# Two transformer layers on one core: a new order for the first transfers and norms, and order tables by segment

## The chip, the cores and the metric

The kernel runs on one core of a Trainium2 chip. The time is the device time of one execution in microseconds (us); lower is better. The engines of a core are TensorE (PE in the profile), VectorE (DVE), ScalarE (ACT), GpSimd (POOL) and SyncE (SP). SP and ACT issue the transfers (DMAs) from the chip's main memory. PE multiplies; only DVE and ACT bring results out of its accumulators, the PSUM banks.

## What is computed

One attention block and one gated feed-forward block, twice in a row with the same weights, over a sequence of 2048 rows of width 512:

```
x = x + attention(layernorm(x)) @ wo      # 32 heads of width 16; a row sees itself and the 255 rows before it
x = x + (sigmoid(g) * u) @ w_down         # g = layernorm(x) @ w_gate, u = layernorm(x) @ w_up, width 1792
```

The layernorm has no scale and no offset and adds 1e-5 to the variance. Queries, keys and values are three slices of `layernorm(x) @ wqkv`; scores are scaled by 1/4.

## The kernel before

**Tiles.** The 2048 rows are 16 tiles of 128; four tiles are a group. x stays in on-chip memory (`xsb`), and so do all weights. A tile's path is: statistics of x on DVE (`BATCH_NORM_STATS2`, L589, then the aggregate, L590; for the first four tiles also the addition of 1e-5, L592), the power -1/2 on POOL (L598, L599), the normalised tile on DVE (L617), its transpose (four PE matmuls at L638 and a copy, L666 on ACT or L668 on DVE; later tiles go by a transposing DMA), then the products for queries (L703), keys (L734) and values (L770). A key tile is copied out and split into even and odd heads by two DVE products (L749).

**Score visits.** Attention runs in 77 visits per layer, 154 in all, each a block of small score matmuls (L1029, L1040, L1050) into four PSUM banks (`Sps`), one exponential of 128x2048 on ACT (L1082, 1.88 us) and mask products on DVE (L960). The values products (L1109) follow when a half tile's exponentials and masks are done. Then come the normalisation by the row sums, the output product (L893), the addition into x (L899), the second norm, the gate and up products (L798), tanh on ACT (L816) and the product on DVE (L824), and the down product (L862) with its addition into x (L871) and, in the second layer, the store (L878).

**The order is planned by the program that writes the kernel.** `Plan` simulates the engines while the instructions are emitted: each task has a set of engines, a duration written by hand, dependencies and a priority; when an engine is free in the plan, the ready task with the lowest priority number is emitted there next. On the chip each engine executes in the emitted order, and waits where something it needs is late. So every constant of the plan (durations, `LAND` and `SLACK` for the landing of transfers, `COLD`, `SWITCH`, `PACE`) acts on the time only through the order. `Net.pick` fills PE: when a visit is due (`pace` after the last one, or as soon as the last exponential is done and there is nothing else) its scores are emitted; otherwise a unit of dense products is chosen by `rank`. With nothing to do it emits `keep_warm` matmuls (L1292) whose results are not used. The tables before are two, one for visits 0 to 23 and one for the rest (`PRIO`, `SLACK`, `RANK`; `LATE_...`); `PACE` has a spacing of 1600 ns for visits 0 to 11, 2511 to visit 23, then 2682 in the first layer and 3207 in the second.

**The first transfers** (`loads`, all issued at L455): x tile 0, x tile 1, x tiles 2 and 3, then the key weights and the query weights; each is halved, one half on SP's queue and one on ACT's. The value weights (512 KB) are whole on ACT's queue. Then SP's queue alone brings x tiles 4 to 7, `wo`, x tiles 8 to 11, the gate and up weights, and, after a planned delay, x tiles 12 to 15 and the down weights in seven parts. The first key and query units work tile by tile (three key chunks, two query chunks); the others need all four tiles.

**Gate and up by groups of tiles** (`glu_units`, `GLU`): `GLU[1][OPT["g2"]]` is [4, 4, 4, 2, 2] in the second layer, so its last four tiles are two groups of two with matmuls of 256 columns.

Of the kernel before, what the change touches and what calls it, by code (L numbers as in the profile page):

```python
# [12 lines left out]
P = 128  # L13
# [43 lines left out]
def pool_ns(n):  # L57
# [5 lines left out]
GLU = [[[1] * 4 + [4], [1] * 4 + [2] * 2, [1] * 6 + [2], [1] * 8, [2] * 4, [1] * 2 + [2] * 3, [2] * 2 + [4]], [[4] * 3 + [2, 1, 1], [4] * 3 + [2, 2], [4] * 4]]  # L63
PACE = [2682, 3207, 1600, 2511, 23.52]
# [6 lines left out]
COLD = 5200  # L71
SWITCH = 96
LAND = 1230
RATE = ((3300, 330.0), (5300, 160.0), (1e9, 345.0))
# [7 lines left out]
PRIO = dict(st_x0=7.13, ap_x0=2.72, xt_x0=3.36, st_x1=-0.44, ap_x1=1.86, xt_x1=6.58, st_x=18.87, ap_x=6.56,  # L82
    xt_x=2.0, st_p=7.13, ap_p=4.46, xt_p=0.81, st_g=2.23, ap_g=1.32, xt_g=6.14, st_g0=5.97, ap_g0=3.21,
    xt_g0=1.33, tp=5.75, tp_g=-0.06, q=4.0, q0=5.51, q1=4.74, k=1.95, k0=-0.89, k1=-1.49, s=-1.15, s0=5.46,
    s1=3.28, v=0.28, v0=5.43, v1=14.72, vv=5.53, exp=3.64, exp0=4.71, m0=4.61, m00=-0.56, e0=1.11, e00=1.28,
    e1=7.21, e10=6.56, m2=0.64, m20=3.6, th=5.12, mu=-0.12, dn=1.29, add=-0.27, add0=1.8, out=-2.4, mv=5.8,
    mv0=6.23, oq=-2.27, oq0=-0.14, no=4.71, no0=2.61, on=5.93, on0=0.59, vc=9.2, vc0=-0.87)
OPT = dict(gu='SP', g1=1, bk=3, bq=2, wide=0, r0=2, g0=1, g2=1, x0=1, eps=1, hold=0, own=1, ck=0, cq=2,
    turn=2)
SLACK = dict(xt=1208, oq=843, on=211, vc=1208)  # L90
RANK = dict(tp=-1.708, o=-2, lead=14.747, far=7.411, v=9.3, g=1.778, d=1.823, feed=11.672, x3=21097, wd=474,
    go=364)
LATE_PRIO = dict(st_p=-0.04, ap_p=7.96, xt_p=-0.99, st_x=1.07, ap_x=4.81, xt_x=-1.16, st_g=1.75, ap_g=1.19,
    xt_g=2.76, q=3.84, k=4.33, s=4.05, v=0.61, exp=1.12, m0=4.62, e0=2.79, e1=4.39, m2=5.49, th=1.65, mu=2.51,
    dn=2.1, add=0.69, out=0.45, mv=3.49, oq=0.77, no=6.44, on=2.16, vc=0.22)
LATE_SLACK = dict(xt=489, oq=1327, on=2346, vc=897)
LATE_RANK = dict(tp=-2, o=1.576, lead=9.722, far=6.159, v=1.796, g=1.769, d=3.896, feed=7.551, go=1418)

class Late(dict):


    def __missing__(self, name):
        return {"vv": self["v"], "tp": 0, "tp_g": 2}[name] if name in ("vv", "tp", "tp_g") else self[name[:-1]]

# [262 lines left out]
class Net:  # L369
# [74 lines left out]
    def loads(self, A_x, wqkv, wo, w_gate, w_up, w_down):  # L444
# [31 lines left out]
        for t, n in {1: ((0, 1), (1, 1), (2, 2)), 2: ((0, 2), (2, 2)), 3: ((0, 1), (1, 3))}[OPT["x0"]]:  # L476
            ev = load_x(self.xsb[:, t:t + n, :], slice(t, t + n), n, 0, ("SP", "ACT"))
            for i in range(t, t + n):
                self.has_x[i] = ev
        if OPT["wide"]:  # L480
            self.has_wq["q"] = self.has_wq["k"] = both([
                load(self.wq[:, k:k + 2, 0:2 * D], wq_src[:, k:k + 2, 0:2 * D], 4 * P * D * 2, prio=0, queue=q, row=4 * D)
                for k, q in ((0, "ACT"), (2, "SP"))])
        else:
            for w in "kq":
                h = slice("qk".index(w) * D, ("qk".index(w) + 1) * D)
                self.has_wq[w] = both([load(self.wq[:, k:k + 2, h], wq_src[:, k:k + 2, h], 2 * P * D * 2, prio=0, queue=q)
                                       for k, q in ((0, "ACT"), (2, "SP"))])
        self.has_wq["v"] = load(self.wq[:, :, 2 * D:3 * D], wq_src[:, :, 2 * D:3 * D], D * D * 2, prio=0, queue="ACT")
# [14 lines left out]
    def constants(self):  # L504
        nc = self.nc
        nc.gpsimd.memset(self.nhalf[:], -0.5)
# [10 lines left out]
        for i in range(2):  # L517
            self.zeros(0, i)
        self.pl.free["POOL"] = 3000.0
        self.pl.free["SP"] = self.pl.free["ACT"] = 750.0  # L520
        self.pl.at(750.0)
        self.pl.at(1500.0)
        self.pl.free["DVE"] = 3600.0
        self.pl.at(3600.0)
# [11 lines left out]
    def later_constants(self):  # L536
# [23 lines left out]
        for i in range(2):  # L560
            self.vzero[i] = pl.task({"POOL": 800}, lambda e, i=i: self.zeros(1, i), first, prio=8, port=True).done
# [7 lines left out]
    def layer_norm(self, key, t, deps):  # L569
# [15 lines left out]
        def stats(e):  # L585
            if "st" not in box:
                box["st"] = self.take("st")
            st = box["st"][0][:, mine]
            nc.vector.bn_stats(out=st[:, 0:6], in_=self.xsb[:, t, :])  # L589
            nc.vector.bn_aggr(out=st[:, 6:8], in_=st[:, 0:6])  # L590
            if first:
                nc.vector.tensor_scalar(out=st[:, 9:10], in0=st[:, 7:8], scalar1=1e-5, scalar2=None, op0=ALU.add)  # L592
# [29 lines left out]
        a = pl.task({"DVE": 910 + 70 * first}, stats, deps, self.prio["st_" + kind], lambda: "st" in box or self.has("st"))  # L622
# [11 lines left out]
        if alone:  # L634
# [6 lines left out]
            def evac(u):  # L641
                pt = self.tp_view(u.bank)
# [29 lines left out]
    @property  # L672
    def prio(self):
        return PRIO if self.slot < PACE[4] else Late(LATE_PRIO)

    @property
    def slack(self):
        return SLACK if self.slot < PACE[4] else LATE_SLACK

    @property  # L680
    def ranks(self):
        return RANK if self.slot < PACE[4] else LATE_RANK
# [839 lines left out]
```

The softmax here doesn't subtract the row's maximum and nothing guards it: scores larger than these inputs give would overflow.

## Time and profile before

| | us |
|---|---|
| median of 3 runs | 541.87 (541.84 to 542.01) |
| span of the profiled execution, first to last instruction | 539.6 |
| PE busy in the span | 531.1 (98%) |
| DVE busy | 420.5 (78%) |
| ACT busy | 382.3 (71%) |
| POOL busy | 43.4 (8%) |
| first score visit, first matmul at | 13.49 |
| last score visit | 470.77 |

The profiled execution is one execution; its span leaves out about 2.3 us that lie around it in the timed runs. "Busy" for PE takes in the modelled drain of each matmul, so a short gap between two matmuls' starts can be hidden in it; the spacing of starts in the timeline is sharper. A group's "idle before" is the time in which its engine had nothing running just before such an instruction, with what ended it. In the timeline a row is a run of like instructions: start, length, engine, line, operation, operands and how many.

### The profile page before, as it was taken

To read this page: it belongs to the slowest core of one execution; us is meant where nothing else is said; L and a number is where in the kernel's file an instruction comes from. 1 tells how busy PE (TensorE), PEld (TensorE's weight loads), DVE (VectorE), ACT (ScalarE), POOL (GpSimd) and SP (SyncE) were. 2 spreads that over 40 slices of the span, in tenths; PEclk is the share of its full clock that TensorE was granted. 3 is DMA by queue.
4 is the path that set the end of the run, shared out by engine and by line. 5 is a ranking of instruction groups with operands and counts; after the bars stand their busy time and mean duration, and the time that the engine had idled before them with its cause. 6 is when DMAs were issued, how large, how long until landed. Compare 5 with 4: busy or idle time off the path is not lost.

```text
span 539.6 us, 21359 instructions
## 1 busy us (share of the span) xinstructions
PE 531.1 (98%) x9658; PEld 293.0 (54%) x9658; DVE 420.5 (78%) x844; ACT 382.3 (71%) x380; POOL 43.4 (8%) x99
## 2 busy tenths in 40 slices
PE   8999999999999999999999999999999999999997
PEld 8446755855767444544444444544444444455873
DVE  6999999789878997798977789778677785674442
ACT  4989989878888687776778767787667866540330
POOL 5301110001000110101100010101000000000000
PEclk9999999999999999999999999999999999999999
DMA  8890334232421323143110622117211241132001
GB/s 260 317 227 15 43 72 57 50 61 63 72 52 33 72 51 60 36 101 59 32 35 14 105 51 47 38 42 108 54 45 28 60 72 50 24 70 58 2 11 39
DMA packets 95067, 36.23 MB, mean 67 GB/s; under 512 B 78336, under 2 KB 93952, under 8 KB 94976
## 3 DMA queue, kind: packets, MB, share of 16 engines
q1 hardware_dynamic: 93600, 33.56, 29.9%
q8 instruction: 75, 1.23, 1.0%
q10 hardware_dynamic: 1376, 1.31, 0.8%
q14 instruction: 16, 0.13, 0.1%
HBM read 9.70 MB, written 2.10 MB: 22 GB/s over the span
## 4 chain that ended last, share of the span: by engine, by line
PE 89%; DVE 5%; ACT 2%; DMA 1%; issue 1%; POOL 0%; SPq 0%; ACTq 0%; POOLq 0%
PE bank L798 37%; PE bank L862 18%; PE bank L1109 9%; PE Sps L1029 7%; PE bank L893 5%; PE bank L734 4%; PE bank L770 3%; PE bank L703 3%; PE Sps L1040 2%; ACT PTring L1082 1%; DMA wq<-in_A_wqkv_dram 1%; DVE kTp L749 1%; DVE st L589 1%; DVE PTring L960 1%; DVE edge L960 1%
## 5 line engine op out<-in xcount | busy, mean ns | idle before, releaser
L1082 ACT ACTIVATE PTring<-Sps 128x2048 bf16<-128x2048 f32 (+1 forms) x122 | 226.0, 1852 | 63.2 <-PE Sps L1029 59.2
L798 PE MATMUL bank<-xnT,wu 128*128 128x512 bf16 (+2 forms) x728 | 128.2, 297 | 0.0
L798 PE MATMUL bank<-xnT,wg 128*128 128x512 bf16 (+2 forms) x728 | 128.2, 298 | 0.0
L862 PE MATMUL bank<-wd,hT 128*128 128x512 bf16 (+2 forms) x462 | 109.9, 373 | 0.0
L824 DVE SCALAR_TENSOR_TENSOR hT<-hT,bank 128x256 bf16<-128x256 bf16 (+1 forms) x154 | 80.8, 537 | 34.0 <-ACT hT L816 21.2
L816 ACT ACTIVATE hT<-bank 128x256 bf16<-128x256 f32 (+1 forms) x154 | 71.1, 482 | 48.5 <-PE bank L798 47.8
L798 PEld LDWEIGHTS <-wg 128*128 128x128 bf16 x728 | 60.7, 98 | 36.7 <-issue 2.3
L798 PEld LDWEIGHTS <-wu 128*128 128x128 bf16 x728 | 61.4, 98 | 34.5 <-issue 2.5
L1082 ACT ACTIVATE edge<-Sps 128x2048 bf16<-128x2048 f32 (+1 forms) x32 | 56.6, 1770 | 17.3 <-PE Sps L1040 17.3
L862 PEld LDWEIGHTS <-hT 128*128 128x128 bf16 x462 | 43.0, 98 | 46.4 <-issue 2.2
L668 DVE CAST OTs<-bank 128x512 bf16<-128x512 f32 x59 | 43.0, 729 | 21.5 <-PE bank L1109 21.1
L960 DVE TENSOR_TENSOR PTring<-PTring,mask 128x1024 bf16<-128x1024 bf16 x64 | 43.7, 684 | 12.3 <-ACT PTring L1082 12.1
L1109 PE MATMUL bank<-PTring,Vaug 128*32 128x64 bf16 (+1 forms) x2880 | 52.0, 203 | 0.0
L1109 PEld LDWEIGHTS <-Vaug 128*32 128x32 bf16 x2880 | 44.0, 97 | 12.0 <-issue 10.4
L1029 PE MATMUL Sps<-qT,kTp 32*128 32x256 bf16 (+3 forms) x1216 | 47.4, 248 | 1.2 <-ACT PTring L1082 1.1
L598 POOL TENSOR_SCALAR st<-st 128x2 f32<-128x2 f32 (+1 forms) x33 | 10.7, 325 | 443.6 <-DVE st L590 443.6
L589 DVE BATCH_NORM_STATS2 st<-xsb 128x6 f32<-128x512 bf16 x64 | 43.9, 686 | 1.7 <-DMA xsb<-in_A_x_dram 1.2
L1109 PE MATMUL bank<-edge,Vl 128*32 128x64 bf16 x1024 | 44.4, 193 | 0.1
L960 DVE TENSOR_TENSOR edge<-edge,maske 128x1024 bf16<-128x1024 bf16 x60 | 40.3, 682 | 3.4 <-ACT edge L1082 3.3
L1029 PEld LDWEIGHTS <-kTp 32*128 32x128 bf16 x1216 | 18.2, 92 | 45.4 <-issue 43.5
L1109 PE MATMUL bank<-edge,Vh 128*32 128x64 bf16 x896 | 40.8, 193 | 0.0
L960 DVE TENSOR_TENSOR PTring<-PTring,maskn 128x1024 bf16<-128x1024 bf16 x56 | 38.2, 682 | 0.0
(73 smaller groups left out, 522.0 us busy)
## 6 DMA issues: line engine op xcount, KB each, us to landing
Vl<-Vaug SPq DMA_DIRECT2D x32, 68.0 KB, 2.4
out_dram<-xsb SPq DMA_DIRECT2D x15, 128.0 KB, 2.1
Vh<-Vaug SPq DMA_DIRECT2D x28, 68.0 KB, 2.5
wg<-in_B_w_gate_dram SPq DMA_DIRECT2D x2, 896.0 KB, 9.7
wu<-in_B_w_up_dram SPq DMA_DIRECT2D x2, 896.0 KB
wd<-in_B_w_down_dram SPq DMA_DIRECT2D x7, 256.0 KB, 5.3
xsb<-in_A_x_dram SPq DMA_DIRECT2D x6, 256.0 KB, 7.4
wq<-in_A_wqkv_dram ACTq DMA_DIRECT2D x2, 256.0 KB, 4.5
```

Source lines behind the costliest of these rows:

```text
L589: nc.vector.bn_stats(out=st[:, 0:6], in_=self.xsb[:, t, :])
L668: self.nc.vector.tensor_copy(out=out, in_=in_)
L734: return [(mm_ns(w), lambda kt=kt, o=o: nc.tensor.matmul(self.banks[bank][:, o:o + w], lhsT=self.wq[:, kt, D + cq * P:D + cq * P + P], rhs ...
L798: return [(mm_ns(w), lambda i=i, j=j, fc=fc, wt=wt, kt=kt: self.nc.tensor.matmul(pt[:, i, j, :], lhsT=wt[:, kt, fc * P:(fc + 1) * P], rhs= ...
L816: self.nc.scalar.activation(out=self.hT[:, ch[0] * GW:ch[0] * GW + size], in_=pt, func=AF.Tanh, scale=0.5)
L824: self.nc.vector.scalar_tensor_tensor(out=h, in0=h, scalar=1.0, in1=pt, op0=ALU.add, op1=ALU.mult)
L862: nc.tensor.matmul(self.banks[bank][:, 0:w], lhsT=self.hT[:, at:at + P], rhs=self.wd[:, fc, d], start=fc == 0, stop=fc == FC - 1)
L893: return [(mm_ns(D), lambda c=c: nc.tensor.matmul(self.banks[bank][:], lhsT=b[0][:, c, :], rhs=self.wot[:, c, :], start=c == 0, stop=c == ...
L960: done = pl.task({"DVE": dve_bf_ns(1024)}, lambda e: nc.vector.tensor_tensor(out=r, in0=r, in1=m.to_broadcast([P, 16, HP]), op=ALU.mult), ...
L1029: nc.tensor.matmul(self.sps[:, m, o:o + n * HP], lhsT=kTp[32 * m:32 * m + 32, i, tt, e, :], rhs=self.qT[32 * m:32 * m + 32, i, q0:q0 + n * ...
L1082: nc.scalar.activation(out=out, in_=src, func=AF.Exp, scale=scale)
L1109: nc.tensor.matmul(o, lhsT=Va[:, c0:c0 + 32], rhs=p(h), start=k == 0 or t == 0, stop=k == len(parts) - 1 or t == 0, tile_position=(0, 32 * g))
```

## The change

The first transfers are x tile 0, x tile 1, key weights, x tiles 2 and 3, query weights, value weights, each halved over SP and ACT (the value weights too). In the plan these land at fixed times (`ARRIVE`) and no longer by a modelled rate. The addition of 1e-5 and the aggregate of the first four tiles become a DVE task of their own (`moments`), so that other work can be emitted between the statistics and them; no instruction is added by this. The zeroing of `Vl` (six POOL memsets, L534) moves from the kernel's first instructions to behind the fourth tile's power on POOL. The `keep_warm` matmuls read a zeroed stretch of `hT` (one DVE memset) in place of the identity that POOL makes, may start 450 ns earlier in the plan, and go singly in the first 10 us. The tables of priorities, landing slack, ranks and spacing are looked up by the visit (`SEGMENTS`, entries every five visits, most of them empty): the spacing is 622 ns for visits 0 to 11, 2218 to 24, 2702 to 79, and about 3017 from 85 on. x tiles 12 to 15 are planned at 33.5 us in place of 21.1, the seven down-weight parts 4.8 us apart from there in place of 1.9. The last four tiles of the second layer are one group of four. Planned durations of scores, values and mode switches are a little longer. The diff, cut to its core:

```diff
--- before.py
+++ after.py
-GLU = [[[1] * 4 + [4], [1] * 4 + [2] * 2, ...], [[4] * 3 + [2, 1, 1], [4] * 3 + [2, 2], [4] * 4]]
-PACE = [2682, 3207, 1600, 2511, 23.52]
+GLU = [[[1, 1, 1, 1, 2, 2], [1, 1, 1, 1, 2, 2], [1, 1, 1, 1, 2, 2], ...], [[4, 4, 4, 2, 1, 1], [4, 4, 4, 1, 1, 2], [4, 4, 4, 4]]]
-COLD = 5200
-SWITCH = 96
+ARRIVE = dict(x0=3200, x1=4050, k=6100, x2=6600, q=8000, v=9600)
+COLD = 6000
+SWITCH = 100
-RATE = ((3300, 330.0), (5300, 160.0), (1e9, 345.0))
+RATE = ((9200, 40.0), (1e9, 345.0))
-PRIO = dict(st_x0=7.13, ap_x0=2.72, xt_x0=3.36, st_x1=-0.44, ap_x1=1.86, xt_x1=6.58, st_x=18.87, ap_x=6.56,
...
-OPT = dict(gu='SP', g1=1, bk=3, bq=2, wide=0, r0=2, g0=1, g2=1, x0=1, eps=1, hold=0, own=1, ck=0, cq=2,
-    turn=2)
-SLACK = dict(xt=1208, oq=843, on=211, vc=1208)
-RANK = dict(tp=-1.708, o=-2, lead=14.747, far=7.411, v=9.3, g=1.778, d=1.823, feed=11.672, x3=21097, wd=474,
-    go=364)
...
-LATE_SLACK = dict(xt=489, oq=1327, on=2346, vc=897)
-LATE_RANK = dict(tp=-2, o=1.576, lead=9.722, far=6.159, v=1.796, g=1.769, d=3.896, feed=7.551, go=1418)
+OPT = dict(gu='SP', g1=1, bk=3, bq=2, wide=0, r0=2, g0=2, g2=2, x0=1, eps=1, hold=0, own=1, ck=0, cq=2, turn=2,
+    split=0, mo=0, r1=0, near=0)
+RANK = dict(x3=33548.83335140428, wd=1211.7000995894928)
+SEGMENTS = {
+    0: (False, dict(st_x0=13.863, ap_x0=3.152, ..., st_x1=3.154, ap_x1=7.542, ..., st_x=14.008,
+        ap_x=13.772, ...), dict(xt=2480, oq=333, on=656, vc=2033),
+        dict(tp=-12.366, o=-7.523, lead=12.467, far=66.411, v=2.907, g=58.132, d=22.245, feed=32.11,
+        x3=33548.83335140428, wd=1211.7000995894928, go=147.06927590305332), 622.2),
...
+    12: (False, {}, {}, {}, 2218.12),
...
+    25: (True, dict(...), dict(xt=205, oq=2779, on=3180, vc=6577), dict(tp=25.318, o=-33.126, lead=9.136, far=25.67, v=1.764,
+        g=13.215, d=13.271, feed=-39.311, go=2154.735913081243), 2702.16),
...
+    80: (False, {}, {}, {}, 2591.1),
+    85: (False, {}, {}, {}, 3017.42),
+    90: (False, dict(oq=-4.09), {}, dict(o=-30.75, lead=9.62, v=1.47), 2875.9),
+    95: (False, dict(oq=-3.007), {}, dict(o=-33.126, lead=9.136, v=1.764), 3017.42),
...
+    115: (False, dict(xt_x=13.72, m0=9.31), {}, {}, 2984.3),
+    120: (False, dict(xt_x=10.765, m0=5.963), {}, {}, 3017.42),
...
+}
+def segments():
+    out, now = {}, [Late(), {}, {}, 0]
+    for slot, (new, prio, slack, rank, pace) in SEGMENTS.items():
+        now = [Late(prio) if new else Late({**now[0], **prio}), {**now[1], **slack}, {**now[2], **rank}, pace]
+        out[slot] = now
+    return out
@@ loads
-        for t, n in {1: ((0, 1), (1, 1), (2, 2)), ...}[OPT["x0"]]:
-            ev = load_x(self.xsb[:, t:t + n, :], slice(t, t + n), n, 0, ("SP", "ACT"))
...
-            for w in "kq":
-                h = slice("qk".index(w) * D, ("qk".index(w) + 1) * D)
-                self.has_wq[w] = both([load(self.wq[:, k:k + 2, h], wq_src[:, k:k + 2, h], 2 * P * D * 2, prio=0, queue=q)
-                                       for k, q in ((0, "ACT"), (2, "SP"))])
-        self.has_wq["v"] = load(self.wq[:, :, 2 * D:3 * D], wq_src[:, :, 2 * D:3 * D], D * D * 2, prio=0, queue="ACT")
+        def at(name, parts):
+            done, landed = Event(), Event()
+            pl.at(ARRIVE[name], landed.fire)
+            when_all(parts + [landed], done.fire)
+            return done
...
+        def tiles(name, t, n):
+            self.has_x.update(dict.fromkeys(range(t, t + n), at(name, [
+                first(self.xsb[z:P:2, t:t + n, :], x_src[z][:, t:t + n, :], ("SP", "ACT")[z]) for z in range(2)])))
+        def weights(name, i):
+            h = slice(i * D, i * D + D)
+            self.has_wq[name] = at(name, [first(self.wq[:, k:k + 2, h], wq_src[:, k:k + 2, h], q) for k, q in ((0, "SP"), (2, "ACT"))])
+        tiles("x0", 0, 1)
+        tiles("x1", 1, 1)
+        weights("k", 1)
+        tiles("x2", 2, 2)
+        weights("q", 0)
+        weights("v", 2)
@@ constants
+        nc.vector.memset(self.hT[:, 0:P], 0.0)
...
-        for i in range(2):
-            self.zeros(0, i)
-        self.pl.free["POOL"] = 3000.0
+        self.pl.free["POOL"] = 2000.0
...
-        self.pl.free["DVE"] = 3600.0
+        self.pl.free["DVE"] = 3250.0
@@ later_constants
+        for i in range(2):
+            self.lzero[i] = pl.task({"POOL": 800}, lambda e, i=i: self.zeros(0, i), first, prio=5.5, port=True).done
@@ layer_norm
             nc.vector.bn_stats(out=st[:, 0:6], in_=self.xsb[:, t, :])
+            if not first:
+                nc.vector.bn_aggr(out=st[:, 6:8], in_=st[:, 0:6])
+        def moments(e):
+            st = box["st"][0][:, mine]
             nc.vector.bn_aggr(out=st[:, 6:8], in_=st[:, 0:6])
-            if first:
-                nc.vector.tensor_scalar(out=st[:, 9:10], in0=st[:, 7:8], scalar1=1e-5, scalar2=None, op0=ALU.add)
+            nc.vector.tensor_scalar(out=st[:, 9:10], in0=st[:, 7:8], scalar1=1e-5, scalar2=None, op0=ALU.add)
...
-        a = pl.task({"DVE": 910 + 70 * first}, stats, deps, ...)
+        a = pl.task({"DVE": 694 if first else 910}, stats, deps, ...)
+        if first:
+            a = pl.task({"DVE": 390}, moments, [a.done] + ..., self.prio["ap_" + kind] + 0.1)
@@ prio, slack, ranks, pace
-        return PRIO if self.slot < PACE[4] else Late(LATE_PRIO)
+        return self.tables[0]
...
+    def enter(self, slot):
+        self.slot = slot
+        if slot in self.segments:
+            self.tables = self.segments[slot]
@@ scores, values (planned times only)
-            return pl.count(8 * len(runs)) or 220
+            return pl.count(8 * len(runs)) or 234
-        return n * 56
+        return n * 59.3
@@ pick, keep_warm
-            if spare and work and 1500 <= pl.now < 85000:
+            if spare and work and 1050 <= pl.now < 85000:
...
-        for i in range(4):
-            nc.tensor.matmul(self.banks[bank][:, 0:P], lhsT=self.ident[:], rhs=self.ident[:], start=True, stop=True)
+        n = 1 if pl.now < 10000 else 4
+        for i in range(n):
+            nc.tensor.matmul(self.banks[bank][:, 0:P], lhsT=self.hT[:, 0:P], rhs=self.hT[:, 0:P], start=True, stop=True)
@@ half_values
-                if z and i < 2:
-                    deps.append(self.vzero[i])
+                if i < 2:
+                    deps.append((self.lzero, self.vzero)[z][i])
```

## The prediction, as put on record

> **What bounds the kernel now.** I read first the shares by engine, then the busy time by stretches, then the first 14 us in order of time, then the rows of the groups that the change touches. The shares, and then the stretches (length, busy us and instructions of each engine):
>
> ```profile
> PE 531.1 (98%) x9658; PEld 293.0 (54%) x9658; DVE 420.5 (78%) x844; ACT 382.3 (71%) x380; POOL 43.4 (8%) x99
> ```
>
> ```profile
> 0.00:11.00 11.00, 8.79 (x109) 8.46 (x110) 7.33 (x29) 3.13 (x5) 6.72 (x28) 1.00 0.76 239
> 11.00:50.00 39.00, 37.42 (x567) 19.98 (x564) 36.96 (x86) 36.08 (x39) 8.20 (x20) 1.00 0.74 215
> 50.00:172.00 122.00, 120.56 (x3032) 82.14 (x3030) 106.94 (x228) 106.43 (x114) 7.98 (x16) 1.00 0.33 55
> 172.00:471.00 299.00, 299.00 (x5382) 140.61 (x5380) 237.33 (x440) 218.24 (x188) 18.27 (x32) 1.00 0.28 53
> 471.00:536.00 65.00, 65.00 (x601) 41.64 (x584) 31.50 (x64) 18.39 (x39) 2.20 (x4) 1.00 0.17 36
> 536.00:539.60 3.60, 0.35 (x7) 0.17 (x4) 0.45 (x2) 0.00 (x0) 0.00 (x0) 0.91 0.13 36
> ```
>
> PE is the bound from 172 us to 536 us without a gap (299.00 of 299.00, 65.00 of 65.00). No order can gain there, unless it has fewer matmuls or fewer changes of kind; it can only lose. What an order can gain lies in three places. Up to 11 us PE does little that counts. From 11 to 172 us it stands for 1.58 + 1.44 = 3.0 us by this view; by the spacing of starts in the timeline I count 17 gaps of together 4.6 us, 2.6 up to 50 us and 2.0 behind it, since the view takes some 0.16 us of drain as busy in each. The last 3.6 us are the last addition and store, which the change leaves alone. So the whole purse is about 4.6 us and what the start gives, of 541.87.
>
> The start, in order of time (rows of PE's weight loads left out):
>
> ```profile
> 1.45 4.87 PE L1292 MATMUL bank<-ident 128*128 128x128 bf16 x44 [1.45 <-POOL ident L508]
> 3.28 0.69 DVE L589 BATCH_NORM_STATS2 st<-xsb 128x6 f32<-128x512 bf16 x1 [1.18 <-DMA xsb<-in_A_x_dram]
> ...
> 5.64 0.69 DVE L589 BATCH_NORM_STATS2 st<-xsb 128x6 f32<-128x512 bf16 x1
> ...
> 8.58 0.73 PE L734 MATMUL bank<-xnT,wq 128*128 128x128 bf16 x10 [0.69 <-DMA wq<-in_A_wqkv_dram]
> ...
> 8.84 0.41 DVE L617 TENSOR_SCALAR xn<-xsb,st 128x512 bf16<-128x512 bf16 x1 [0.44 <-POOL st L599]
> ...
> 9.86 1.28 DVE L551 TENSOR_SCALAR maskn<-mask 128x64 bf16<-128x64 bf16 x1 [0.34 <-POOL mask L545]
> ...
> 11.33 0.23 DVE L554 TENSOR_SCALAR mask<-mask,odd 128x64 bf16<-128x64 bf16 x1
> ...
> 13.49 0.40 PE L1029 MATMUL Sps<-qT,kTp 32*128 32x256 bf16 x8
> ```
>
> Two chains meet: the keys' landing at 8.5, for which PE stands, and the norms of four tiles one after another on DVE (the fourth is normalised at 8.84), which lead to the first scores at 13.49.
>
> **The change part by part.** All sums are against the profiled execution: span 539.6 and the 2.3 us around it that make the median of 541.87.
>
> *Key weights ahead of x tiles 2 and 3.* The issues by queue, with KB and us to landing:
>
> ```profile
> xsb<-in_A_x_dram SPq DMA_DIRECT2D x1, 128.0 KB, 3.2
> wq<-in_A_wqkv_dram SPq DMA_DIRECT2D x1, 256.0 KB, 5.5
> wq<-in_A_wqkv_dram ACTq DMA_DIRECT2D x1, 256.0 KB, 3.6
> ```
>
> They were issued at 2.32, 3.02 and 2.73, so SP had landed 256 KB (x tiles 0 to 3) at 5.5 and 512 KB (with its half of the keys) at 8.5; ACT had its 512 KB at 6.3. Now the keys end after 384 KB of each queue: halfway, an estimate of 7.0 on SP and 5.5 on ACT. The wait before 8.58 (two key products had run at 7.62, so 0.9 us) should go. But x tiles 2 and 3 then end where the keys ended: 6.3 on ACT and, by the same queue rows, as late as 8.5 on SP; if the two queues share evenly and 1024 KB take as long on both, nearer to 7. DVE began with tile 2 at 5.64. Its work until then in the new order (two statistics of 0.69, two moments of 0.18 + 0.15, two normalisations of 0.40, gaps) lasts to about 7.1, so a landing at 7.0 costs little and one at 8.5 costs 1.5 us in the fourth tile. Cheaper by the split: the first normalisation no longer waits for tile 1's aggregate (it ran at 5.32; POOL had finished at 5.09), 0.2 us.
>
> What does PE get from this? By 11.0 it had issued 16 transposes and 29 products of 56 ns, 2.5 us of work. With keys at 7.0 and queries earlier, tiles 0 and 1 alone give 8 transposes, 24 key and 16 query products, 2.7 us; with tile 2 in time some 1.3 us more. So between 0 and 1.5 us is gained on PE, and up to 1.5 us lost if tile 2 lands at 8.5 and the delay passes on. I take a gain of 0.4.
>
> [...] No row shows a rate gained by two queues: 239 GB/s with both in the first 11 us, 389 from 11 to 20 us with SP's alone.
>
> *Warm-up.* PE's first 44 filler matmuls start at 1.45 and come 107 ns apart; the spacing turns to 56 ns at 6.4. Only the first four transposes (6.12 to 6.5) are useful work at half rate: 4 x 51 ns = 0.2 us, in the start's bounds above. The filler now waits for a DVE memset (0.11 us, in DVE's wait of 1.18 us for x), no longer for POOL at 1.44.
>
> *The zeroing of Vl* was 1.61 us on POOL at 1.34, beside nothing. It now lies behind 9 us, where POOL's memsets run already and DVE is full: `maskn` (L551) took 1.28 us beside them, the like product L554 0.23. If that is the memsets' doing, six more cost DVE between 0 and 1.6 us, and DVE has only 39.00 - 36.96 = 2.0 us free up to 50 us. I take 0.2 on the path, since most DVE work there is not what PE waits for. [...] The zeros themselves are needed at 21, when the first copies to `Vl` are issued.
>
> *Tables by segments.* Before, the early gaps follow the supply of normalised tiles, and those behind 50 us mostly a score visit that waits for the last exponential:
>
> ```profile
> PE Sps L1029 <- ACT PTring L1082: 1.1, 4, 0.4
> PE bank L638 <- DVE xn L617: 0.5, 2, 0.3
> ```
>
> Earlier scores and a spacing that holds more filler behind the visits can remove them; new spacings can also put a visit where its exponential is late. I bound the part by -4.6 (all gaps gone) and +2.6 (new gaps in the 364 us from 172, now full, at a quarter of the rate of the 161 us before: 4.6 x 364 / 161 / 4), and take half of the purse, -2.3. DVE at 95% up to 50 us is why not all goes. Changes of kind cost too: from 26.67, eleven products of 216 ns reach 29.05, and the scores start at 29.14, so about 0.1 us per change. Six of 63 values passes stand apart from scores; the same number more or fewer is 0.6 us either way; taken 0. The down weights, issued up to 34.6 before, are planned until 62.6 and land 5.3 us later by their row, at 68; the first down product ran at 59.0. Gate and up products (48 to 76 for the first four tiles) cover that; without the cover, the wait would be 9 us less what is at hand, so this is a condition, priced at 0.
>
> *One group of four at the end.* In the second layer 224 matmuls of 256 columns become 112 of 512. By the timeline four of 256 take 521.01 - 520.57 = 0.44 us, four of 512 take 479.75 - 478.89 = 0.86: 56 x 0.437 - 28 x 0.864 = 0.3 us saved. All four tiles must now be normalised before the last 24 us of gate and up; the output product of the last tile ran at 490.3, 34 us before the last down block, and the shorter spacing brings it forward (70 visits x about 0.2 us and more at the start), so PE has the group before it as filler. Priced at nothing beyond the 0.3.
>
> Sum: -0.4 (start) + 0.2 (POOL beside DVE) - 2.3 (gaps) - 0.3 (group) = -2.8. **Forecast: 541.9 - 2.8 = 539.1.**
>
> **Rivals.**
>
> *Tiles 2 and 3 come late (slower).* The price: landing at 8.5, statistics at 8.6 in place of 5.64, the fourth tile normalised at about 11.5 in place of 9.25, first scores 1.5 us later; DVE, 95% busy up to 50 us, can't make it up, and the early gaps stay. +1.5 (start) + 0.2 - 0.3 = 543.3. It decides when tile 2's later half lands after about 7.1. For it: SP's row above. Against: PE has key, query and value products of tiles 0 and 1 to do meanwhile.
>
> *No change.* The gaps move and keep their sum, since DVE sets them; only the group and the start remain: 541.9 - 0.7 + 0.2 = 541.4. [...]
>
> *All gaps go.* -4.6 - 0.3 - 1.0 (start) + 0.2 = -5.7: 536.2. For it: 172 to 536 us shows that an order can keep PE full for 364 us. Against: the early gaps follow from DVE's load.
>
> **Numbers.** Forecast 0.57 (537.3 to 540.5), all gaps gone 0.10, no change 0.16, tiles late 0.17. Faster by over 0.2% (below 540.8): 0.57 + 0.10 and a little of the third case, 0.70. Within 0.2%, about what a measurement of this kernel can tell from no change: 0.15. Slower: 0.15. The range from 536.4 to 543.4 takes in the late tiles at their price and nearly all gaps gone; it leaves out new gaps in the full stretch and a start better than its bound.
>
> **What would show it.** Keys: PE's first L734 before 7.6 with no wait on `wq`. Tile 2: the third L589 at about 7 (forecast) or 8.6 (late tiles), and the first scores below or above 13.5. Tables: PE's missing time from 11 to 172 us at about half of 3.0 by the stretches, and none behind. Group: 512-column matmuls alone at the end. I am wrong if PE stands between 172 us and the end, if the down weights are waited for at 60 to 70 us, or if DVE's products beside POOL's memsets grow.

## The result, and the profile after

The changed kernel takes 542.34 us (median of 12 runs, 540.47 to 543.56) against 541.90 us for the kernel before in the same rounds (12 runs, 540.68 to 542.60). The ratio is 1.0008, interval 0.9996 to 1.0019: **no change that can be measured**. The forecast of 539.1 was wrong. The time lies in the range that was given, but none of the gain came. The profiled execution took 542.07 us, with a span of 540.36.

The shares of the changed kernel, and its busy time by the same stretches as before:

```profile
PE 529.0 (98%) x9536; PEld 279.7 (52%) x9536; DVE 411.0 (76%) x820; ACT 385.9 (71%) x377; POOL 43.6 (8%) x99
```

```profile
0.00:11.00 11.00, 6.39 (x83) 5.97 (x84) 5.75 (x26) 2.46 (x3) 2.96 (x11) 1.00 0.78 240
11.00:50.00 39.00, 37.02 (x582) 20.55 (x580) 35.74 (x87) 36.24 (x39) 12.20 (x37) 1.00 0.57 188
50.00:172.00 122.00, 120.84 (x2927) 80.20 (x2924) 106.39 (x225) 107.09 (x112) 9.39 (x18) 1.00 0.36 64
172.00:471.00 299.00, 299.00 (x5638) 142.52 (x5636) 238.34 (x445) 226.37 (x202) 18.16 (x32) 1.00 0.30 57
471.00:536.00 65.00, 65.00 (x310) 29.88 (x309) 24.02 (x39) 13.73 (x23) 0.93 (x2) 1.00 0.07 21
```

Read it by stretches. From 172 to 536 us PE is as full as before (299.00 and 65.00). PE's busy time in all is 2.1 us less than before (529.0 against 531.1), but that is no work saved: the first stretch alone has 2.4 us less (6.39 in place of 8.79). PE stands in the start, and the timeline of the start says for what (rows of PE's weight loads and most others left out):

```profile
1.04 3.78 PE L1366 MATMUL bank<-hT 128*128 128x128 bf16 x42 [1.04 <-DVE hT L561]
...
7.47 1.11 PE L807 MATMUL bank<-xnT,wq 128*128 128x128 bf16 x17
...
8.35 1.29 DVE L645 BATCH_NORM_STATS2 st<-xsb 128x6 f32<-128x512 bf16 x2 [1.58 <-DMA xsb<-in_A_x_dram]
...
10.57 0.93 DVE L677 TENSOR_SCALAR xn<-xsb,st 128x512 bf16<-128x512 bf16 x2 [0.39 <-POOL st L659]
...
10.78 0.62 PE L776 MATMUL bank<-xnT,wq 128*128 128x128 bf16 x8 [2.20 <-DMA wq<-in_A_wqkv_dram]
...
11.63 0.39 PE L700 MATMUL Sps<-ident,xn 128*128 128x128 bf16 x4
...
12.10 0.29 DVE L605 TENSOR_SCALAR maskn<-mask 128x64 bf16<-128x64 bf16 x1 [0.34 <-POOL mask L599]
...
16.16 0.40 PE L1102 MATMUL Sps<-qT,kTp 32*128 32x256 bf16 x8
```

The key products (L807) run at 7.47 without a wait; before, ten of twelve ran at 8.58. That much is as planned. But DVE then stands 1.58 us for x tiles 2 and 3, and PE 2.20 us for the query weights. The first scores come at 16.16, **2.67 us later** than the 13.49 of before. The transfers behind it were issued at 2.05 and 2.33 (keys on ACT's and SP's queue), 2.69 and 2.98 (x tiles 2 and 3), 3.39 and 3.69 (queries). KB and us to landing, from three narrow stretches:

```profile
wq<-in_A_wqkv_dram ACTq DMA_DIRECT2D x1, 256.0 KB, 3.5
wq<-in_A_wqkv_dram SPq DMA_DIRECT2D x1, 256.0 KB, 3.9
...
xsb<-in_A_x_dram ACTq DMA_DIRECT2D x1, 128.0 KB, 4.1
xsb<-in_A_x_dram SPq DMA_DIRECT2D x1, 128.0 KB, 5.3
...
wq<-in_A_wqkv_dram ACTq DMA_DIRECT2D x1, 256.0 KB, 5.7
wq<-in_A_wqkv_dram SPq DMA_DIRECT2D x1, 256.0 KB, 7.0
```

So the keys had landed at 5.5 and 6.3, the last half of tiles 2 and 3 at 8.3, and the last half of the queries at 10.7.

### The profile page after: what moved, and what is told of

It reads as the page before. It is cut to its first block, busy times and chain, and to the rows that moved or that the text cites. A ratio compares the mean times of both kernels' runs of the same rounds, so it can differ in the third digit from the quotient of the medians.

```text
span 540.4 us, 21116 instructions
## 1 busy us (share of the span) xinstructions
PE 529.0 (98%) x9536; PEld 279.7 (52%) x9536; DVE 411.0 (76%) x820; ACT 385.9 (71%) x377; POOL 43.6 (8%) x99
## 4 chain that ended last, share of the span: by engine, by line
PE 90%; DMA 3%; ACT 3%; DVE 2%; issue 1%; SPq 1%; POOL 0%; ACTq 0%
PE bank L871 37%; PE bank L935 18%; PE bank L1182 8%; PE Sps L1102 7%; PE bank L966 5%; PE bank L776 4%; PE bank L807 4%; PE bank L843 4%; PE Sps L1113 2%; DMA xnT<-xn 2%; ACT PTring L1155 1%; DMA wq<-in_A_wqkv_dram 1%; SPq L527 1%; DVE st L645 0%; DVE PTring L1033 0%
## 5 line engine op out<-in xcount | busy, mean ns | idle before, releaser
L871 PE MATMUL bank<-xnT,wu 128*128 128x512 bf16 (+2 forms) x672 | 125.0, 308 | 0.0
L871 PE MATMUL bank<-xnT,wg 128*128 128x512 bf16 (+2 forms) x672 | 123.6, 309 | 0.4 <-DMA xnT<-xn 0.4
L897 DVE SCALAR_TENSOR_TENSOR hT<-hT,bank 128x512 bf16<-128x512 bf16 (+1 forms) x140 | 78.9, 576 | 44.7 <-PE bank L871 36.4
L889 ACT ACTIVATE hT<-bank 128x512 bf16<-128x512 f32 (+1 forms) x140 | 69.8, 514 | 56.3 <-PE bank L871 55.8
L935 PE MATMUL bank<-wd,hT 128*128 128x512 bf16 (+2 forms) x462 | 108.8, 373 | 0.0
L871 PEld LDWEIGHTS <-wu 128*128 128x128 bf16 x672 | 55.9, 98 | 40.5 <-issue 2.5
L871 PEld LDWEIGHTS <-wg 128*128 128x128 bf16 x672 | 55.0, 98 | 41.8 <-issue 3.0
L736 DVE CAST OTs<-bank 128x512 bf16<-128x512 f32 x50 | 36.4, 729 | 13.8 <-PE bank L1182 13.4
```

The costliest lines, as they stand in the source:

```text
L736: self.nc.vector.tensor_copy(out=out, in_=in_)
L871: return [(mm_ns(w), lambda i=i, j=j, fc=fc, wt=wt, kt=kt: self.nc.tensor.matmul(pt[:, i, j, :], lhsT=wt[:, kt, fc * P:(fc + 1) * P], rhs= ...
L889: self.nc.scalar.activation(out=self.hT[:, ch[0] * GW:ch[0] * GW + size], in_=pt, func=AF.Tanh, scale=0.5)
L897: self.nc.vector.scalar_tensor_tensor(out=h, in0=h, scalar=1.0, in1=pt, op0=ALU.add, op1=ALU.mult)
L935: nc.tensor.matmul(self.banks[bank][:, 0:w], lhsT=self.hT[:, at:at + P], rhs=self.wd[:, fc, d], start=fc == 0, stop=fc == FC - 1)
```

## The experiments

Two things changed together, the start and the tables. So the start was changed with the tables kept, and the other way round.

**The transfers alone, in the new kernel.** The two lines are exchanged, nothing else; the planned landing times stay, so every engine executes the same instructions in the same order, and only the landings move.

```diff
         tiles("x1", 1, 1)
-        weights("k", 1)
         tiles("x2", 2, 2)
+        weights("k", 1)
         weights("q", 0)
```

> The changed kernel with nothing but the third and fourth transfer of each queue exchanged again: x tiles 2 and 3 before the key weights; the order on PE, DVE and POOL is the same instruction for instruction. Late-tiles theory: tile 2's later half lands at about 6 in place of 8.3, first scores at 14 to 15 in place of 16.2, and the time falls by 1 to 2 us against the changed kernel. Rival (the start's loss is taken up by later slack, or the queries' landing at 10.7 sets the start anyway): less than 0.4 us.

Measured: 540.15 us (539.75 to 540.65), ratio 0.9968 (0.9957 to 0.9980). This beats both kernels: its interval does not touch that of the changed kernel (0.9996 to 1.0019). Its start:

```profile
6.72 1.28 DVE L645 BATCH_NORM_STATS2 st<-xsb 128x6 f32<-128x512 bf16 x2
...
7.52 1.11 PE L807 MATMUL bank<-xnT,wq 128*128 128x128 bf16 x17
...
9.10 0.62 PE L776 MATMUL bank<-xnT,wq 128*128 128x128 bf16 x8 [0.47 <-DMA wq<-in_A_wqkv_dram]
...
9.94 0.39 PE L700 MATMUL Sps<-ident,xn 128*128 128x128 bf16 x4
...
14.48 0.40 PE L1102 MATMUL Sps<-qT,kTp 32*128 32x256 bf16 x8
```

DVE takes the statistics of tiles 2 and 3 without waiting, and the key products still run at 7.52, as early as with the keys ahead, since the norms and transposes of tiles 0 and 1 last until then anyway (tile 1's transposes run from 7.07 to 7.45). The keys were quick in this execution (7.35 at the latest). In the four other profiles with x ahead of the keys, of kernels that follow, their later half landed between 8.27 and 8.95, and PE stood for it up to 1.56 us; yet the first scores came between 14.53 and 15.33 there, still ahead of the changed kernel's 15.80 and 16.16 (its two profiles). Here the first scores are 1.68 us earlier than in the changed kernel, and the last PE instruction starts 2.06 us earlier (534.43 against 536.49).

**The transfers alone, in the kernel before.** The third and fourth transfer of each queue are exchanged in what is issued; the plan, and with it the order on PE, DVE and POOL, is that of before.

```diff
-        self.has_x, self.has_wq = {}, {}
-
+        self.has_x, self.has_wq, sent = {}, {}, {"SP": [], "ACT": []}
...
-            q = {"SP": nc.sync, "ACT": nc.scalar}[queue]
-            return pl.dma(ns, nbytes, lambda: q.dma_start(out=dst, in_=src), (), prio, after, queue, bulk=(queue, row)).done
+            q, mine, i = {"SP": nc.sync, "ACT": nc.scalar}[queue], sent[queue], {2: 3, 3: 2}.get(len(sent[queue]), len(sent[queue]))
+            mine.append(dict(out=dst, in_=src))
+            return pl.dma(ns, nbytes, lambda: q.dma_start(**mine[i]), (), prio, after, queue, bulk=(queue, row)).done
```

> The kernel before with nothing but the third and fourth transfer of each queue exchanged: key weights before x tiles 2 and 3; the order on PE, DVE and POOL is that of before, instruction for instruction. Late-tiles theory: third statistics at about 8.3 in place of 5.64, first scores about 1.5 us later than 13.49, and a time of 1 to 2 us over before. Rival (the keys' earlier landing, which ends PE's wait at 8.5, pays for it): within 0.4 us of before.

Measured: 544.44 us (542.93 to 544.58), ratio 1.0041 (1.0028 to 1.0053); first scores at 16.18 in place of 13.49. Here the third statistics stand ahead of tile 1's normalisation in DVE's order, so a tile that has long landed waits behind one that has not:

```profile
8.12 0.69 DVE L589 BATCH_NORM_STATS2 st<-xsb 128x6 f32<-128x512 bf16 x1 [2.30 <-DMA xsb<-in_A_x_dram]
...
9.13 0.41 DVE L617 TENSOR_SCALAR xn<-xsb,st 128x512 bf16<-128x512 bf16 x1
...
9.60 0.61 PE L638 MATMUL Sps<-ident,xn 128*128 128x128 bf16 x4 [2.15 <-DVE xn L617]
```

After this PE's clock was down to half for 3.4 us. The columns are the stretch, its length, the busy us and instructions of PE, PEld, DVE, ACT and POOL, the granted clock, the DMA share and GB/s:

```profile
9.60:13.00 3.40, 3.40 (x33) 3.40 (x34) 2.55 (x8) 1.10 (x2) 2.58 (x12) 0.50 1.10 357
```

So in both orders the new sequence of transfers brings the first scores about 2.7 us later. In this kernel much of the 2.5 us goes with the clock: the four executions with a mean granted clock of 0.996 or 0.997 took 544.38 to 544.58 us, the one with 0.999 took 542.93. As far as one execution tells, some 1.5 us go with the clock and 1.0 is left for the late data, hardly clear of the spread of the kernel before (up to 542.74 in the same rounds).

**The tables alone.** The new kernel with the transfers, the landing model, the warm-up, the zeroing and the norms of before:

```diff
-COLD = 6000
+COLD = 5200
-RATE = ((9200, 40.0), (1e9, 345.0))
+RATE = ((3300, 330.0), (5300, 160.0), (1e9, 345.0))
...
-        tiles("x0", 0, 1)
...
-        weights("v", 2)
+        for t, n in ((0, 1), (1, 1), (2, 2)):
+            ev = load_x(self.xsb[:, t:t + n, :], slice(t, t + n), n, 0, ("SP", "ACT"))
...
```

> The changed kernel with the start of before put back: transfers, planned landings, warm-up, zeroing of Vl and norms as before; tables by segment, planned durations and the last group of four stay as changed. Late-tiles theory (the new start costs about 1.7 us and the tables with the group gain about as much): first scores at about 13.5 us and a time 1 to 2 us under before, 540 to 541. Tables theory (the new tables gain nothing, whatever the start): the same as before within 0.5 us, with gaps of PE from 11 to 172 us that again sum to 4 us or more.

Measured: 549.47 us (549.07 to 550.43), ratio 1.0141 (1.0125 to 1.0156), with the first scores as early as before (13.5). This run could not do what it was made for: with other due times the same tables write out another order, and that one is 7 us worse from end to end. It cannot price the tables as they stand in the changed kernel, and neither expectation was met.

**Due times that are true.** Since the planned landings (tiles 2 and 3 at 6.6, queries at 8.0) were so far off, the measured ones were put in the plan: first in the changed kernel, then in the kernel with x ahead of the keys.

```diff
-ARRIVE = dict(x0=3200, x1=4050, k=6100, x2=6600, q=8000, v=9600)
+ARRIVE = dict(x0=3230, x1=4400, k=6300, x2=8300, q=10750, v=11850)
+ARRIVE = dict(x0=3390, x1=4360, k=7350, x2=5480, q=9050, v=10470)
```

> The changed kernel with the landings that its trace shows as the plan's due times (x0 3230, x1 4400, keys 6300, x2 8300, queries 10750, values 11850 ns in place of 3200, 4050, 6100, 6600, 8000, 9600), so that the order fits what comes. Due-times theory (the order was planned for transfers that come 2 us earlier, and that is the loss): 1 us or more under the changed kernel, 541 or less. Late-tiles theory (the data are late, whatever the order): first scores stay at about 16 and the time changes by less than 0.5 us.

> The kernel with x before the keys again, and the landings of its own trace as due times (x0 3390, x1 4360, x2 5480, keys 7350, queries 9050, values 10470 ns). Due-times theory (true due times give the better start): first scores before 14.5 us and 540 or less. Fitted-tables theory: a better start, first scores at 14 or before, and still 543 or more, with the loss behind 50 us.

Measured: 547.75 us (547.04 to 548.05), ratio 1.0105 (1.0091 to 1.0119), and 542.92 us (542.78 to 543.38), ratio 1.0027 (1.0015 to 1.0039). Both are slower than the kernels with the false times, by some 5 and 2.8 us. The start is not what lost it. In the first kernel the first scores came at 15.66 in place of 16.16; in the second at 15.12 in place of 14.48, but within the 14.48 to 15.33 of the other kernels with x ahead of the keys. From the first scores to the last PE instruction the two take 526.9 and 522.3 us, where the kernels with the false times take 520.3 and 519.9. So true due times did not help, against the due-times theory of both runs, and the first run's rival (less than 0.5 us) failed too; the second run's rival, the fitted tables, had the size nearly right (543 or more) and the earlier start wrong. In the second kernel PE stands 1.3 us for an exponential's edge part ahead of two score blocks between 11 and 60 us.

**A due time that is a little different.** To see whether truth matters or only the fit, one planned landing was moved by 100 ns in the kernel with x ahead of the keys.

```diff
-ARRIVE = dict(x0=3200, x1=4050, k=6100, x2=6600, q=8000, v=9600)
+ARRIVE = dict(x0=3200, x1=4050, k=6100, x2=6700, q=8000, v=9600)
```

> The kernel with x before the keys again, and in the plan alone x tiles 2 and 3 due 100 ns later (6700 in place of 6600). The transfers are the same, and PE's order is the same for its first 2304 instructions (some 75 us) and dealt anew behind that. Fitted-tables theory (the tables suit one order only; whatever moves the plan slightly loses the gain, which is what happened where the old start and the true landings were put in): 543 or more, 3 us or more over x before the keys. Rival (those two lost by their start or their due times, not by the new deal): within 1 us of x before the keys, 541 or less.

Measured: 545.46 us (544.68 to 546.10), ratio 1.0075 (1.0057 to 1.0093), 5.3 us above the kernel with 6600. PE's order is the same for some 75 us and differs behind that. From 172 to 471 us PE is no longer full, here first, and then a kernel with the fitted order (the next experiment):

```profile
172.00:471.00 299.00, 296.01 (x5530) 141.16 (x5529) 237.17 (x443) 223.98 (x199) 19.33 (x32) 1.00 0.30 57
```

```profile
172.00:471.00 299.00, 299.00 (x5618) 142.22 (x5616) 238.05 (x443) 225.36 (x201) 17.33 (x31) 1.00 0.30 57
```

Of the 2.99 us that are missing, 1.81 are one stop inside a values pass, for which the profile has no releaser ("issue"):

```profile
227.94 0.19 PE L1182 MATMUL bank<-PTring,Vaug 128*32 128x64 bf16 x1
229.95 0.21 PE L1182 MATMUL bank<-PTring,Vaug 128*32 128x64 bf16 x3 [1.81 <-issue]
```

The run with the tables alone has two of the kind (1.39 us at 228.06, 2.42 at 467.27). So the tables fit one sequence of planned events. Here a plan that differs by a tenth of a microsecond gave another order, and a time 5 us off.

**The values' other half on ACT's queue.** In both profiles of the changed kernel SP's queue has the later landings (the queries at 10.7, on ACT's queue at 9.1; in the second profile x tiles 2 and 3 took 5.5 us from issue to landing on SP's queue, 3.8 on ACT's). Here SP's half of the value weights is issued on ACT's queue, in the kernel with x ahead of the keys.

```diff
-        def first(dst, src, queue):
-            q = {"SP": nc.sync, "ACT": nc.scalar}[queue]
+        def first(dst, src, queue, values=False):
+            q = {"SP": nc.scalar if values else nc.sync, "ACT": nc.scalar}[queue]
...
-            self.has_wq[name] = at(name, [first(self.wq[:, k:k + 2, h], wq_src[:, k:k + 2, h], q) for k, q in ((0, "SP"), (2, "ACT"))])
+            self.has_wq[name] = at(name, [first(self.wq[:, k:k + 2, h], wq_src[:, k:k + 2, h], q, name == "v") for k, q in ((0, "SP"), (2, "ACT"))])
```

> The kernel with x before the keys again, and SP's half of the value weights issued on ACT's queue, as before the change, so that x tiles 4 to 7 follow the query weights on SP at once; the order on PE, DVE and POOL is the same. Shared-engines theory (two queues bring no more bytes; only the order of bytes counts): the query weights land at the same time, x tiles 4 to 7 up to 1 us earlier, the value weights 1 to 1.5 us later, and the time moves by less than 0.3 us, as neither is waited for. Rival (SP's half delays x tiles 4 to 7 and with them DVE's second group): 0.3 to 0.8 us less.

Measured: 540.25 us (540.01 to 541.60), ratio 0.9974 (0.9965 to 0.9984), the same as without the edit. The queries landed at 8.84 and 9.12 (8.87 and 9.05 without it), the first scores came at 14.53 (14.48), and in the first 11 us 238 GB/s were moved (240).

**The zeroing of `Vl` back at the start**, in the kernel with x ahead of the keys; the tasks stay in the plan and emit nothing.

```diff
+        self.zeros(0, 0), self.zeros(0, 1)
...
-            self.lzero[i] = pl.task({"POOL": 800}, lambda e, i=i: self.zeros(0, i), first, prio=5.5, port=True).done
+            self.lzero[i] = pl.task({"POOL": 800}, lambda e, i=i: None, first, prio=5.5, port=True).done
```

> The kernel with x before the keys again, and the six memsets of Vl back among POOL's first instructions; every other engine has the same order. Port theory (memsets beside DVE slow it in the stretch where it is full): DVE's small products at 12 to 13 us shorter, the first scores up to 0.5 us earlier, the time down by 0.2 us or more. Rival (POOL's memsets cost DVE nothing that PE waits for): no change beyond 0.15 us against x before the keys.

Measured: 540.83 us (540.31 to 541.49), ratio 0.9983 (0.9974 to 0.9991). That is 0.7 us above x ahead of the keys (0.9968), where one side expected less time and the other the same; the two intervals overlap, so the difference is not shown. The sign of the forecast's +0.2 was wrong. `maskn`, the product that was taken as the sign of it, is short when the six memsets lie beside it, and long when they do not and those of `Vaug` lie there; first with the zeroing late (x ahead of the keys), then with the zeroing early:

```profile
10.45 0.29 DVE L605 TENSOR_SCALAR maskn<-mask 128x64 bf16<-128x64 bf16 x1 [0.34 <-POOL mask L599]
```

```profile
10.23 1.02 DVE L605 TENSOR_SCALAR maskn<-mask 128x64 bf16<-128x64 bf16 x1 [0.35 <-POOL mask L599]
```

Later products of the masks (L610, L611) are in turn 0.39 and 0.32 us with the zeroing late and 0.18 and 0.18 with it early, so the mask products take together 1.8 against 2.0 us. From the first scores to the last PE instruction both kernels take 519.9 us. The profiled execution's later end (535.22 against 534.43) is all ahead of the first scores: the keys landed at 8.95 on SP in place of 7.35, and PE stood 1.56 us for them.

```profile
9.00 1.12 PE L807 MATMUL bank<-xnT,wq 128*128 128x128 bf16 x17 [1.56 <-DMA wq<-in_A_wqkv_dram]
```

Whether the early memsets delay the keys, or the landing only scatters, is open.

**One group of four in the kernel before.**

```diff
-OPT = dict(..., g0=1, g2=1, ...)
+OPT = dict(..., g0=1, g2=2, ...)
```

> The kernel before with nothing but the second layer's last four tiles as one group of four; the order is that of before up to the last 2% of PE's instructions. The prediction's step: 0.3 us less (541.6), PE without a gap after 471 us, since the group before covers the wait for tiles 14 and 15. Rival (with the old, slower spacing the four tiles are ready too late): PE stands for 1 us or more near 497 us and the time rises by as much.

Measured: 541.57 us (540.70 to 542.51), ratio 0.9998 (0.9990 to 1.0007), not to be told from no change. The profiled execution has the same PE order as before up to the group. Its first scores came 0.85 us late; the keys landed at 9.39 on SP (8.54 before), though the first transfers are the same. From the last score visit to PE's last start it took 65.07 us against 65.36: the 0.3 us of the forecast.

**The changed kernel again**, in the rounds of the three kernels above and without an edit, for its first transfers and its clock.

> The changed kernel once more, for its second profile. Clock theory (PE stands 2.4 us for the query weights, and in some executions the granted clock falls to half for a while after it, as it did where the keys went third in the old order): times spread over 2 us or more, and an execution with a stretch of half clock before 15 us lies 1 us or more over one without. Rival: the clock stays full in every profile and the spread has another cause.

Measured: 541.78 us (539.95 to 544.13), ratio 1.0001 (0.9987 to 1.0016). In this profile, by the spacing of its matmuls (56 ns), the clock was full from 6.39 on and did not fall back, nor did it in the first profile once it was full. But both profiled executions have a mean granted clock of 0.999, and the other executions do not all. Of the 22 of the changed kernel (both sets of rounds), 13 have 0.999 or 1.000 and a median of 541.71 us; nine have 0.993 to 0.997 and a median of 543.25. A mean of 0.997 is what 3.4 us at half clock would make of 540 us (an estimate: 0.5 x 3.4 / 540 = 0.3%). So the spread and the 1 us or more of the clock theory are there; where in those executions the clock was down, no profile shows. All 37 executions with x ahead of the keys, and all 52 of the kernel before in the rounds of the experiments, have 0.999 or 1.000. The clock adds to the loss, but it is not the whole of it: with a full clock the changed kernel still takes 541.7 us, against 540.2 to 540.8 for the same order with x ahead of the keys.

This time the queries landed at 9.86, and tiles 2 and 3 at 8.47: with the queries earlier, the tiles were what PE waited for in the end (0.34 us at 11.26), and the first scores came at 15.80.

```profile
8.57 1.29 DVE L645 BATCH_NORM_STATS2 st<-xsb 128x6 f32<-128x512 bf16 x2 [1.59 <-DMA xsb<-in_A_x_dram]
...
11.26 0.40 PE L700 MATMUL Sps<-ident,xn 128*128 128x128 bf16 x4 [0.34 <-DVE xn L677]
```

**What the profiles show together.** In kernels that execute the same order, lateness in the start arrives at the end nearly undiminished: of the 0.85 us between the first scores with x ahead of the keys and those with the early zeroing, 0.79 are left at the last PE instruction. Times of the profiled executions, in us:

| kernel | third tile's transposes | first scores | last PE instruction | from first scores to it |
|---|---|---|---|---|
| before | 9.43 | 13.49 | 536.13 | 522.64 |
| before, group of four | 10.28 | 14.34 | 536.87 | 522.53 |
| before, keys third | 11.81 | 16.18 | 539.04 | 522.86 |
| changed | 11.63 | 16.16 | 536.49 | 520.33 |
| changed, again | 11.26 | 15.80 | 535.89 | 520.09 |
| x ahead of keys | 9.94 | 14.48 | 534.43 | 519.95 |
| and values on ACT | 10.00 | 14.53 | 534.58 | 520.05 |
| and early zeroing | 10.80 | 15.33 | 535.22 | 519.89 |

The new order needs 4.53 or 4.54 us from the third tile's transposes to the first scores in each of these profiles, the old one 4.06 (4.37 where the clock was down). The transposes in turn start in the new order at the latest of three moments: the landing of tiles 2 and 3 and 2.79 us (8.47 to 11.26, in the changed kernel's second profile), that of the keys and 1.85 us (8.95 to 10.80, early zeroing; 1.73, from 8.80 to 10.53, in the kernel with the due time moved by 100 ns), that of the queries and 0.89 us (10.74 to 11.63, changed kernel, and 9.05 to 9.94, x ahead of the keys). And the new order is 2.2 to 3.0 us shorter behind the first scores.

## Why the prediction was wrong, step by step

**The start (forecast -0.4, measured +2.67 to the first scores).** This is the step that failed. It was right that the keys come earlier (the estimate of 7.0 on SP was even too late: 6.3) and that the key products lose their wait. It was wrong in two places.

- *Tiles 2 and 3.* Two ends were in hand: 8.5 us by SP's own row, and 7 by an even sharing of the two queues, and the forecast took the second. Measured: 8.26 and, again, 8.47. The rows of this very queue were nearer than the reckoning with a shared rate. In the first profile the tiles alone would have put the third tile's transposes at 8.26 + 2.79 = 11.05, 1.62 us later than the 9.43 of before. The rival's price of 1.5 was too low by its own figures: the fourth tile normalised at 11.5 in place of 9.25 is 2.25 us, and it was normalised at 11.50.
- *The queries.* The text said "queries earlier". But nothing was moved from ahead of them, and they landed at 10.74 (9.86 in the second profile), after 9.97 before. In the new order their products stand ahead of the third tile's transposes, so PE waited for them (2.20 us) with the transposes behind. They, not the tiles, set the 11.63: another 0.58 us. The other 0.47 of the 2.67 is the longer way from there to the first scores (4.53 for 4.06).

Not all of the 2.67 is lost: before the first scores PE now does 5.57 us of transposes and dense products that count, where it did 4.86 (an estimate: their number times the usual spacing, 56 ns, and 216 for the three of 512 columns). The net price of the start is 2.67 - 0.71 = 2.0 us. The forecast had no term for the clock either; in the nine executions with a lower mean clock it goes with some 1.5 us more.

The rate was not raised: 240 GB/s in the first 11 us after, 239 before. So what the keys gain is paid for by the transfers behind them, and the sum is a loss, since the bytes that were pushed back are needed sooner than those that were brought forward (2.79 us lie between the landing of x tiles 2 and 3 and the third tile's transposes, 1.85 between that of the keys and the transposes).

**POOL beside DVE (forecast +0.2).** Wrong in sign and of no weight: 0.2 us less in the mask products with the zeroing late (1.8 against 2.0). The slow products change places, they do not add up: `maskn` took 0.29 us with the zeroing late and 1.02 with it early, L610 and L611 took 0.39 and 0.32, and then 0.18 and 0.18.

**Gaps (forecast -2.3).** Right in sign, and too large. From the first scores to 172 us, PE's missing time by the stretches fell from 3.02 to 2.35 us, 0.7 in place of the half that was forecast. Short waits that the stretches do not see come in by the table: behind the first scores the changed kernel is 522.64 - 520.33 = 2.31 us shorter, of which 0.71 is the work done ahead and 0.29 the group of four, so 1.3 is left for gaps and changes of kind. In the four other profiles of this order the rest is 1.5 to 1.75. How much of it is gaps and how much changes of kind, this does not part. The view that was named as the test (11 to 172 us, half of 3.0) shows 3.14, because 0.79 us of the new standing in the start falls behind 11 us. No stall appeared between 172 us and the end, and none for the down weights, so the forecast's conditions held.

**One group of four (forecast -0.3).** Measured 0.29, by the kernel that has this edit alone.

The sum of these is +2.0 + 0 - 1.3 - 0.3 = +0.4, as the two profiled executions differ at PE's last start (+0.36; the gaps were found as the rest of it); the medians differ by +0.4 and, in the second rounds, -0.1. Two rivals named a time nearer to it. *Tiles 2 and 3 come late* is what happened in the start, at more than its price; it named 7.1 as the point from which it decides, and the landing was 8.3. Its sum of 543.3 was too high because it held that the early gaps stay, and they shrank. *No change* had about the right time (541.4) for the wrong reason, which is luck: the gaps did not keep their sum.

That the loss is the transfers' and not the tables' is shown by the exchange of the two lines, the same order of work with other landings: 0.9968 against 1.0008. The lower clock of some executions belongs to this loss: with x ahead of the keys it was seen in none of 37. What the tables give apart from their own start is shown only from the first scores on, since the attempt to put them on the old start made another order.

## What to carry to other kernels

Order transfers by the work that lies between each landing and the point where all are needed. Here it was 2.79 us behind x tiles 2 and 3, 1.85 behind the keys, 0.89 behind the queries, so that keys ahead of x put off the longest chain. The queue's own row gave one landing and an even share of the rate another, and in both profiles the row was the nearer (8.5 by the row, 7 by the share; 8.26 and 8.47 measured). And an order that was fitted to planned times is fitted to those numbers, right or wrong: a due time that is corrected, or moved by 100 ns, is a new order that has to be fitted and measured again.

## What the runs showed of the hardware

**The first landings scatter from execution to execution**: the last half of the keys landed at 8.54 and 9.39 in two kernels with the same first transfers, the queries at 10.74 and 9.86 in two executions of the changed kernel. The two halves of the keys, issued 0.3 us apart, landed up to 2.7 us apart (6.25 and 8.95 in the kernel with early zeroing, 6.33 and 8.54 before); in the kernel with x ahead of the keys, where they were issued at 2.75 and 2.76, they landed at 7.10 and 7.35. In each of the eleven other profiles the queue that issued its third transfer later, by 0.26 to 0.29 us, also landed its half of the keys later; that is SP's queue in six of them and ACT's in five, and in the five kernels with x ahead of the keys it changes. With the table above, a microsecond there is nearly a microsecond at the end. How much of the 2 to 4 us between the fastest and the slowest run of a kernel comes from it, and how much from the clock, is not parted.

**The clock.** The filler matmuls start 107 ns apart at first and 56 ns apart later. From PE's first matmul to that change it took 5.0 us in the kernel before (1.45 to 6.44), 2.7 in the changed one (1.04 to 3.71) and 5.4 in the same kernel's second profile (1.04 to 6.39). The view's granted clock is 1.00 in these stretches; that it is the clock all the same is the author's estimate, from the 33 matmuls that took 3.40 us, 103 ns each, at the granted clock of 0.50 above. There, after PE had stood for 2.15 us, the clock fell to half for 3.41 us by the spacing, from 9.62 to 13.04. The changed kernel's stand of 2.20 us, a little later in the start, had no such effect (a granted clock of 1.00 up to 11 us and from 11 to 50). What sends the clock back after one stand and not after another is open; by the mean clocks above (0.993 to 0.997), a like loss happens in nine of 22 executions of the changed kernel and in four of five of the kernel before with the keys third.

**Stops with nothing to wait for.** In two kernels PE stops for 1.4 to 2.4 us (and in the changed kernel with true landings for 0.5 and 0.9) in the middle of a values pass, a run of small matmuls of 64 columns, with "issue" in the profile. No profile of the order of before or of the changed order has such a stop. A transfer of 16 KB on the instruction queue starts within 1.2 us of the start of each of the three long ones, but such transfers come throughout (75 in the kernel before); whether PE's instructions had not arrived is not settled by these runs.
